# Moving the row-threshold add of a fused attention and FFN kernel from GpSimd to VectorE, with an order of instructions drawn from sixty

## Chip, cores and metric

One core of a Trainium2 chip. The metric is device time in microseconds of one execution; less is better.

## The reference, cut to what matters

```python
# q, k, v: 8 batches, 8 heads, 576 positions, 64 wide;  tau = 0.02
scores = scale * q @ k^T
thresh = max(scores, axis=-1) - tau
scores = where(scores >= thresh, scores, -1e9)
attn   = softmax(scores) @ v
# then an FFN on the 4608 rows: RMS norm, silu(x @ w_gate) * (x @ w_val) @ w_out
```

Only the threshold of each row, its maximum less tau, is touched by the change. It decides which scores survive.

## The kernel before

The kernel describes its work as a list of operations with an engine, an estimated cost, a priority and dependences. A small simulation in the kernel, `order_ops`, plays them through and gives the order in which every engine gets its instructions. I call the end time that this simulation arrives at the *reckoning*. There are 144 steps, each with the scores of two heads for 128 rows. The part of a step that matters (cut):

```python
def emit_softmax(s, so):
    for h in range(2):                      # VectorE: scores out of PSUM, negated and scaled, row minimum into mx
        nc.vector.tensor_tensor_reduce(out=ssb[a][:, h], in0=s_ps[h][...], in1=zrow, scale=-1.0 / 8.0,
                                       scalar=3.0e38, op0=ALU.add, op1=ALU.min, accum_out=mx[m][:, h:h + 1])
    def nthr(o):                            # GpSimd: the threshold of both heads, 128x2
        nc.gpsimd.tensor_scalar(out=nth[m], in0=mx[m], scalar1=tau, scalar2=None, op0=ALU.add)
    tn = add("POOL", COST["pool_tiny"], s - 4, [ttr_of[s, 0], ttr_of[s, 1]], nthr)
    # way "p", ScalarE: prelu(bias=nth) with a huge slope, then exp
    # way "g" (one head of every other step from step 16 on): ScalarE exp(bias=nth) into esb,
    #     GpSimd "mask" wsb = (ssb <= nth), GpSimd "take" wsb = wsb * esb
    ...
...
seq = order_ops(ops, {"R": 4})
for o in seq:
    o.fn(o)
```

`s_ps` has one buffer per head, so the next step's score matmuls wait until VectorE has copied this step's (in the trace of before a score group takes 1.17 us when nothing holds it and 1.91 us where it waits for the copy).

## Time and profile before

| | before |
|---|---|
| median | 568.11 us (567.13 to 568.92) |
| TensorE (PE), VectorE (DVE), ScalarE (ACT), GpSimd (POOL) busy | 98%, 75%, 80%, 57% |
| the threshold add | 144 on GpSimd, 220 ns each |
| score copy, mask, take | 754 ns, 1726 ns, 1278 ns each |

The groups' columns are: line, engine, operation, tiles written and read, shapes, count, then busy time in us and the mean in ns. A busy PE is not a full PE: a score group of eight matmuls counts as busy from its first to its last even when it is held in between (all of the 1.91 us above).

### The profile page before, as it was taken

Reading aid. Unit: us, or ns where it says so; the run is one execution under the profiler, and the core shown is the slowest. Engines: PE = TensorE matmul, PEld = TensorE weight load, DVE = VectorE, ACT = ScalarE, POOL = GpSimd, SP = SyncE. Lnnn points to the kernel's source line nnn. Section 1 sums busy time; section 2 is a strip of 40 time slices with the busy share of each in tenths; the row PEclk is TensorE's granted clock in tenths of the full one; section 3 lists DMA queues with packets and bytes.
Section 4 is the critical chain, followed back from the end, with each engine's and each line's share of the span. In section 5 each row is a group of like instructions: output and inputs, shape, how many; then the busy total and the mean of one; then the engine's idle time right before and its main releaser. Section 6 shows DMA issues by size and latency. Waiting matters only on the chain.

```text
span 568.3 us, 13686 instructions
## 1 busy us (share of the span) xinstructions
PE 558.4 (98%) x5000; PEld 334.7 (59%) x5000; DVE 427.2 (75%) x1093; ACT 457.4 (80%) x739; POOL 322.4 (57%) x462
## 2 busy tenths in 40 slices
PE   8999999999999999999999999999999999999997
PEld 4666766767676555555555555545555455454674
DVE  4899977969958588758895789659875886586354
ACT  4999899999878787979898898778978897884332
POOL 2378946976747457666766658555666555551000
PEclk9999999999999999999999999999999999999999
DMA  8999998769994686999876799789887565633211
GB/s 187 250 289 282 178 195 184 161 132 202 167 202 104 136 159 149 177 177 187 178 160 148 142 186 181 161 168 162 174 167 184 88 96 86 178 81 44 84 37 38
DMA packets 270019, 88.98 MB, mean 157 GB/s; under 512 B 252544, under 2 KB 262272, under 8 KB 269952
## 3 DMA queue, kind: packets, MB, share of 16 engines
q1 hardware_dynamic: 267168, 86.02, 74.1%
q0 software_dynamic: 1600, 1.57, 1.8%
q8 instruction: 39, 0.64, 0.5%
q10 hardware_dynamic: 1184, 0.52, 0.3%
q14 instruction: 28, 0.23, 0.1%
HBM read 37.75 MB, written 9.44 MB: 83 GB/s over the span
## 4 chain that ended last, share of the span: by engine, by line
PE 89%; DVE 3%; DMA 2%; issue 2%; ACT 2%; POOL 1%; SPq 0%; DVEq 0%; POOLq 0%; ACTq 0%
PE s_ps L566 28%; PE ring L792 16%; PE ring L797 16%; PE ring L853 14%; PE ring L697 6%; PE ring L303 2%; PE ring L693 2%; DVE ssb L589 2%; DMA qkn<-in_q_dram 1%; PE s_ps L831 1%; PE s_ps L853 1%; PE ring L659 1%; PE s_ps L797 1%; PE ring L364 1%; DMA stage<-in_q_dram 1%
## 5 line engine op out<-in xcount | busy, mean ns | idle before, releaser
L589 DVE CUSTOM_DVE_ANT_0 ssb<-s_ps,zrow 128x576 f32<-128x576 f32 x288 | 207.8, 754 | 67.7 <-PE s_ps L566 60.5
L607 ACT ACTIVATE ssb<-ssb,nth 128x576 f32<-128x576 f32 x224 | 165.9, 766 | 32.4 <-POOL nth L596 32.1
L566 PE MATMUL s_ps<-qkt 64*128 64x288 f32 x1024 | 170.2, 429 | 1.4 <-DVE mx L589 1.1
L566 PEld LDWEIGHTS s_ps<-qkt 64*128 64x128 f32 x1024 | 96.2, 186 | 53.5 <-DVE mx L589 16.2
L640 POOL TENSOR_SCALAR wsb<-ssb,nth 128x576 f16<-128x576 f32 x64 | 110.5, 1726 | 9.7 <-DMA wt<-wsb 2.9
L792 PE MATMUL ring<-xnT,wg 128*128 128x512 f16 (+1 forms) x548 | 112.9, 328 | 0.4 <-DVE sl L809 0.4
L797 PE MATMUL ring<-xnT,wv 128*128 128x256 f16 (+1 forms) x544 | 111.4, 327 | 0.6 <-ACT qTv L472 0.3
L596 POOL TENSOR_SCALAR nth<-mx 128x2 f32<-128x2 f32 x144 | 31.6, 220 | 133.9 <-DVE mx L589 120.6
L809 DVE SCALAR_TENSOR_TENSOR sl<-th,ring 128x512 f32<-128x512 f32 (+1 forms) x137 | 75.9, 554 | 25.9 <-ACT th L806 24.6
L614 ACT ACTIVATE wsb<-ssb 128x1152 f16<-128x1152 f32 x80 | 92.9, 1161 | 1.9
L806 ACT ACTIVATE th<-ring 128x512 f32<-128x512 f32 (+1 forms) x137 | 66.3, 486 | 28.9 <-PE ring L792 26.4
L853 PE MATMUL ring<-wo,hf 128*128 128x512 f16 x384 | 89.3, 380 | 0.0
L645 POOL TENSOR_TENSOR wsb<-wsb,esb 128x576 f16<-128x576 f16 x64 | 81.8, 1278 | 8.8 <-ACT esb L626 4.4
L814 DVE TENSOR_TENSOR hf<-ring,sl 128x256 f16<-128x256 f32 (+1 forms) x136 | 75.9, 558 | 10.0 <-PE s_ps L566 0.5
L797 PEld LDWEIGHTS <-wv 128*128 128x128 f16 x576 | 52.2, 98 | 42.9 <-issue 12.3
L792 PEld LDWEIGHTS <-wg 128*128 128x128 f16 x576 | 52.0, 98 | 41.0 <-issue 11.6
L853 PEld LDWEIGHTS <-hf 128*128 128x128 f16 x408 | 37.4, 98 | 47.2 <-issue 6.6
L626 ACT ACTIVATE esb<-ssb,nth 128x576 f16<-128x576 f32 x64 | 49.2, 768 | 7.1 <-POOL nth L596 7.0
L697 PE MATMUL ring<-va,wt 128*128 128x65 f16 (+1 forms) x1264 | 52.8, 193 | 0.0
L697 PEld LDWEIGHTS <-wt 128*128 128x128 f16 (+1 forms) x1280 | 48.7, 100 | 3.4
L611 ACT ACTIVATE wsb<-ssb 128x576 f16<-128x576 f32 x64 | 43.6, 681 | 1.6
L693 PE MATMUL ring<-va,wt 128*128 128x130 f16 (+1 forms) x158 | 35.1, 227 | 0.1
(68 smaller groups left out, 448.1 us busy)
## 6 DMA issues: line engine op xcount, KB each, us to landing
vst<-in_v_dram SPq DMA_DIRECT2D x32, 256.0 KB, 3.2
qkn<-in_k_dram SPq DMA_DIRECT2D x31, 256.0 KB, 3.8
out_dram<-osb SPq DMA_DIRECT2D x31, 256.0 KB, 2.6
qkn<-in_q_dram SPq DMA_DIRECT2D x28, 256.0 KB, 4.1
stage<-in_moe_w_gate_dram SPq DMA_DIRECT2D x6, 512.0 KB, 6.6
stage<-in_moe_w_val_dram SPq DMA_DIRECT2D x6, 512.0 KB, 6.3
wt<-wsb SPq DMA_TRANSPOSE x128, 3.1
wo<-in_moe_w_out_dram POOLq DMA_DIRECT2D x4, 384.0 KB, 7.6
```

What stands on the lines that cost most here:

```text
L566: nc.tensor.matmul(s_ps[h][rows, ROW_AT + n * part:ROW_AT + n * part + n], lhs(hs), kT[i][p][h][hs, n * part:n * part + n], start=True, st ...
L589: nc.vector.tensor_tensor_reduce(out=ssb[a][:, h], in0=s_ps[h][:, ROW_AT:ROW_AT + S], in1=zrow, scale=-1.0 / 8.0, scalar=3.0e38, op0=ALU.a ...
L607: nc.scalar.activation(out=ssb[a][:, h], in_=ssb[a][:, h], func=PRELU, scale=-1.0, bias=nth[m][:, h:h + 1], **PRELU_KW)
L614: nc.scalar.activation(out=wsb[s % NW], in_=ssb[a], func=AF.Exp)
L640: nc.gpsimd.tensor_scalar(out=wsb[s % NW][:, h], in0=ssb[a][:, h], scalar1=nth[m][:, h:h + 1], scalar2=None, op0=ALU.is_le)
L645: nc.gpsimd.tensor_tensor(out=wsb[s % NW][:, h], in0=wsb[s % NW][:, h], in1=esb[es], op=ALU.mult)
L697: nc.tensor.matmul(ring[o.slot[0]][rs, at:at + D + 1], w[:, 5 * h + j, rs], va[vi][:, p, 2 * j + h], start=False, stop=(h == 1 and j == 3))
L792: nc.tensor.matmul(ring[o.slot[0]][:, 0:n], wg[d][:, fs], xnT[slot][:, d, 0:n], start=(d == 0), stop=(d == 3))
L797: nc.tensor.matmul(ring[o.slot[0]][:, 0:n], wv[d][:, fs], xnT[slot][:, d, 0:n], start=(d == 0), stop=(d == 3))
L809: nc.vector.scalar_tensor_tensor(out=sl[i][:, 0:n], in0=th[i][:, 0:n], scalar=1.0, in1=ring[g.slot[0]][:, 0:n], op0=ALU.add, op1=ALU.mult)
L814: nc.vector.tensor_tensor(out=hf[hi][:, 0:n], in0=ring[vv.slot[0]][:, 0:n], in1=sl[i][:, 0:n], op=ALU.mult)
L853: nc.tensor.matmul(ring[(first or o).slot[0]], hf[hs[fc][0]][:, 128 * j:128 * (j + 1)], wo[:, fc], start=(fc == 0), stop=(fc == NFC - 1))
```

## The change

The intent: take 31.6 us and a queue off the path from row maximum to ScalarE, and find a better order by drawing.

```diff
-    sp=480.0, sp_v=650.0, sp_w=600.0, sp_tr=1300.0, sp_qk=900.0, sp_tl=630.0,
+    sp=420.0, sp_v=600.0, sp_w=600.0, sp_tr=1300.0, sp_qk=680.0, sp_tl=630.0,
...
+def best_order(ops, ring_sizes):
+    given = [o.prio for o in ops]
+    found = []
+    for seed in list(range(ORDERS)) + [None]:
+        rnd = random.Random(min(found)[1] if seed is None else seed)
+        for o, prio in zip(ops, given):
+            o.prio = prio + (rnd.gauss(0.0, 0.25) if prio > -15 else 0.0)
+        seq = order_ops(ops, ring_sizes)
+        found.append((max(o.end for o in ops), seed))
+    return seq
...
-        def nthr(o):
-            nc.gpsimd.tensor_scalar(out=nth[m], in0=mx[m], scalar1=tau, scalar2=None, op0=ALU.add)
-        tn = add("POOL", COST["pool_tiny"], s - 4, [ttr_of[s, 0], ttr_of[s, 1]], nthr)
+        tns = []
+        for lo, hi in ((0, 1), (1, 2)) if NTH == "EACH" else ((0, 2),):
+            def nthr(o, lo=lo, hi=hi):
+                (nc.gpsimd if NTH == "POOL" else nc.vector).tensor_scalar(
+                    out=nth[m][:, lo:hi], in0=mx[m][:, lo:hi], scalar1=tau, scalar2=None, op0=ALU.add)
+            tns.append(add("POOL" if NTH == "POOL" else "DVE", COST["pool_tiny"] if NTH == "POOL" else NTHC, s - 4, ...))
...
-    seq = order_ops(ops, {"R": 4})
+    seq = best_order(ops, {"R": 4})
...
+ORDERS = 60
+NTH = 'DVE'
+NTHC = 80.0
```

So three things change at once: the engine of the add, the draw, and the issue costs that the reckoning gives to DMAs.

More of the change, by code (lines that the diff above doesn't have):

```diff
@@ L123, in order_ops @@
     return out
+def best_order(ops, ring_sizes):
+    import random
+    given = [o.prio for o in ops]
[7 more added lines that the diff above has]
+    return seq
 @with_exitstack
@@ L593, in emit_softmax @@
             ttr_of[s, h] = add("DVE", COST["ttr"], s - 1, [so, o_c] + exp_of.get(s - NSS, []), ttr)
-        def nthr(o):
-            nc.gpsimd.tensor_scalar(out=nth[m], in0=mx[m], scalar1=tau, scalar2=None, op0=ALU.add)
-        tn = add("POOL", COST["pool_tiny"], s - 4, [ttr_of[s, 0], ttr_of[s, 1]], nthr)
+        tns = []
[3 more added lines that the diff above has]
+                    out=nth[m][:, lo:hi], in0=mx[m][:, lo:hi], scalar1=tau, scalar2=None, op0=ALU.add)
+            tns.append(add("POOL" if NTH == "POOL" else "DVE", COST["pool_tiny"] if NTH == "POOL" else NTHC, s - 4,
+                           [ttr_of[s, h] for h in range(lo, hi)], nthr))
         wfree = [w_read.get(s - NW)]
@@ L614, in ex2 @@
                     nc.scalar.activation(out=wsb[s % NW], in_=ssb[a], func=AF.Exp)
-                pls.append(add("ACT", COST["prelu"], s + 0.5, [tn], prelu))
+                pls.append(add("ACT", COST["prelu"], s + 0.5, [tns[h % len(tns)]], prelu))
                 if ways != "pp":
@@ L627, in ex @@
                                          bias=nth[m][:, h:h + 1])
-                e = add("ACT", COST["exp1"], s + 0.4, [tn, pre.get(("es", es))], ex)
+                e = add("ACT", COST["exp1"], s + 0.4, [tns[h % len(tns)], pre.get(("es", es))], ex)
                 if way == "d":
@@ L646, in take @@
                                                 op=ALU.mult)
-                    mk = add("POOL", COST["mask_g"], s + 0.4, [tn] + wfree, mask)
+                    mk = add("POOL", COST["mask_g"], s + 0.4, [tns[h % len(tns)]] + wfree, mask)
                     st = add("POOL", COST["take_g"], s + 0.4, [e, mk], take)
```

## The prediction

> **What bounds the kernel now.** I read the page from the top: busy shares, the chain that ended last, then the busy time by stretches, and last the groups, the waits and the timeline for the operation that moves.
>
> ```profile
> span 568.3 us, 13686 instructions
> PE 558.4 (98%) x5000; PEld 334.7 (59%) x5000; DVE 427.2 (75%) x1093; ACT 457.4 (80%) x739; POOL 322.4 (57%) x462
> ...
> PE 89%; DVE 3%; DMA 2%; issue 2%; ACT 2%; POOL 1%; SPq 0%; DVEq 0%; POOLq 0%; ACTq 0%
> ```
>
> TensorE is busy for 98% and holds 89% of the chain. GpSimd, from which the change takes work, holds 1% of the chain. A busy PE need not be a full PE, so I looked at stretches next.
>
> ```profile
> 0.00:80.00 80.00, 75.11 (x718) 52.04 (x722) 65.93 (x191) 67.22 (x107) 47.08 (x88) 1.00 1.05 233
> 80.00:180.00 100.00, 99.02 (x1059) 68.70 (x1058) 79.04 (x222) 87.96 (x155) 68.92 (x94) 1.00 0.86 168
> 180.00:510.00 330.00, 329.98 (x2853) 179.62 (x2852) 251.43 (x614) 281.84 (x437) 203.48 (x275) 1.00 0.77 153
> 510.00:568.30 58.30, 54.29 (x377) 34.37 (x375) 30.84 (x70) 20.33 (x43) 2.93 (x6) 0.99 0.20 52
> ```
>
> The columns are the stretch, its length, then the busy time of PE, PEld, DVE, ACT and POOL. From 180 to 510 us PE has no idle time at all. To see whether that is real work, I took from the timeline the start-to-start time of each group of matmuls (eight for scores, four for a gate or value, six for an output, eighteen for attention times values) and compared it with the shortest tenth of the same kind followed by the same kind of work. The excess, counted where it is over 60 ns, is 18.0 us in all: 12.4 us of it starts before 80 us, 3.4 us from 80 to 180 us, and only 2.1 us in the whole rest. So from 180 us PE is truly full, and what an ordering can win lies almost all in the first seventh. There the chain of waits shows it directly:
>
> ```profile
> 18.33 1.91 PE s_ps L566 x8
> ...
> 42.25 1.91 PE s_ps L566 x8
> 47.53 1.91 PE s_ps L566 x8
> ...
> 259.56 1.17 PE s_ps L566 x8
> ```
>
> A score group takes 1.17 us when nothing holds it, 1.91 us where the second head's matmuls wait for VectorE to copy the second head's scores of the step before out of PSUM. Early in the kernel VectorE also copies the weight transposes and transposed keys, so it is the pace-maker there (65.9 of 80 us busy).
>
> Last, the operation that moves and who waits for it:
>
> ```profile
> L596 POOL TENSOR_SCALAR nth<-mx x144: 215/220/227, 10.6 to 511.5; 128x2 f32<-128x2 f32 x144
> ...
>   ACT ssb L607: 32.1, 39
>   ACT esb L626: 7.0, 13
>   POOL wsb L640: 1.6, 2
> ```
>
> The threshold costs GpSimd 144 x 0.220 = 31.6 us, and ScalarE idles 39.1 us in 52 places for it. No PE line is among the waiters: what is lost here is ScalarE's time, and ScalarE is 80% busy.
>
> [...] The trace has near relatives: the accumulator read of one column takes 83 ns, a reciprocal of 128x4 from PSUM 179 ns. I estimate[...] 100 ns taken from the queue. [...] the score copies are uniform (747 to 759 ns) whatever GpSimd does.
>
> **The change part by part.**
>
> Part 1, off GpSimd: -31.6 us of its 322.4 (57% to 51%), and the add no longer queues behind GpSimd's mask (1.73 us) and take (1.28 us). GpSimd isn't on the path except in a few places; one is near 169 us, where the chain runs through mask and take, and PE's attention group at 175 us is 0.84 us late. Worth to the end: at most that 0.8 us, of which I count 0.3.
>
> Part 2, on to VectorE: [...] After 80 us this is hidden: from 80 to 510 us VectorE is busy for 79.0 + 251.4 = 330 of 430 us, so 100 us are free[...]. Before 80 us it isn't: 24 of the steps lie there and VectorE paces the scores; 24 x 0.1 = 2.4 us, of which I count 1.4 us as not covered by waits that it already has.
>
> Part 3, the shorter path from maximum to ScalarE. In the timeline of an undelayed step the accumulator read ends at 259.20, the GpSimd add runs from 259.37 to 259.59, and ScalarE starts at 259.62: 0.42 us. [...] Where GpSimd was occupied the wait is longer: the maximum is there at 251.83, the add starts at 253.96, and ScalarE has idled 0.63 us. Of 39.1 us of ScalarE's waits I expect 25 us to go. On the end this counts only before 80 us, where those waits sum to 4.5 us and ScalarE is busy for 67 of 80 us: I count -1.7 us.
>
> Part 4, the order. Sixty draws with shifts of a quarter of a step (3.9 us pitch, so about 1 us), and the shortest by the ordering's own reckoning. Its reckoning also gets cheaper issue costs for the loads. From 80 us on PE has 5.5 us of stalls to win, before it 12.4 us. Changes between the scores' half-array matmuls and the full-array ones cost some 0.19 us per round trip (scores to gate 335 ns against 235 ns to transposes, gate to scores 309 against 216 ns); there are 132 round trips, and I don't expect more than five to vanish (1 us). The order before was itself tuned, so a draw is on average somewhat worse, and choosing the best of sixty turns that round as far as its reckoning resembles the chip. I count -2.0 us.
>
> Part 5, unchanged: the 7.2 us to the first scores, which wait for loads, and the 4.0 us after the last matmul (564.3 to 568.3), which are an eviction and a store.
>
> Sum: -0.3 + 1.4 - 1.7 - 2.0 = -2.6 us; 568.1 - 2.6 = 565.5 us. The floor for any order of this work is 568.1 - 18.0 = 550.1 us, at 3.2% below, so 2% would need 11.4 of 18 us.
>
> **The rivals.**
>
> Rival A[...]. At the end of the second score copy GpSimd was running something other than the threshold in 16 of 24 steps before 80 us, with 0.33 us to go on the mean over all, and in 47 of 119 later, with 0.18 us. If the add waits each time, VectorE loses 7.9 us before 80 us and 21.5 us after. The latter fits into the 100 us that are free. The former brings VectorE to 65.9 + 2.4 + 7.9 = 76 of 80 us, and with the pacing there I expect 3 to 5 us on the end: 569 to 571 us. [...]
>
> Rival B, the order wins most of the slack: with early score groups at 1.2 to 1.4 us in place of 1.9 us, some 9 us of the 12.4 go and the time is 558 to 560 us. For it: the slack is of the sort that order decides (which copy VectorE takes first). Against it: the copies have to be done all the same, and VectorE is 82% busy there.
>
> Rival C, the reckoning's best isn't the chip's: it knows transfers only as fixed times, while DMA shares are about 1.05 before 80 us. One load a little later stalls PE, as the 1.0 us at 37.4 us does now (transposes held by a load of queries). That gives 568 to 572 us.
>
> **Range and chances.** A chance of a quarter for A and C together and of a sixth for B puts 8 in 10 between 560 and 571 us. Faster by over 2% means below 556.8 us, slower means above 579.5 us; PE's full stretch makes both unlikely: 0.05 faster, 0.92 within 2%, 0.03 slower.
>
> **What would show it.** In the changed trace: no GpSimd threshold, and 144 VectorE ones[...] or a long tail up to 1.7 us where GpSimd is busy (rival A). ScalarE's waits for the threshold near 14 us (part 3). PE's idle time before 80 us below 4.9 us and fewer score groups at 1.9 us (part 4); 180 to 510 us as full as before. I am wrong if PE's stretch after 180 us gets holes, if the round trips change by tens, or if the time before 80 us lengthens.

In the +1.4 us, the 100 ns of VectorE's queue per add are the estimate, set between the 83 and the 179 ns of the two relatives in the trace. Rival A is the case that the add on VectorE waits for the GpSimd instruction that is running.

## More of the kernel before

All runs quoted are fast, with a granted TensorE clock of 0.995 to 1.000. The four calls of experiments ran on four chips (numbers 12, 8, 15 and 5), so kernels of different calls are best compared by their ratios to the kernel before, which ran in every call.

Line numbers differ between the kernels: the add is L596 before and L613 (L614 with a line more) in the later ones.

## The result, and the profile after

The changed kernel takes 573.01 us (572.11 to 574.53, 6 runs) against 568.08 us (6 runs): ratio 1.0092, 95% interval 1.0072 to 1.0113. Ratios here are the mean time of one kernel's fast runs over that of the other's of the same rounds, so not quite the ratio of the medians. It is slower by 0.9%, outside the range of the prediction.

The page of the changed kernel, its head:

```profile
span 571.3 us, 13626 instructions
...
PE 552.9 (97%) x5000; PEld 330.2 (58%) x5000; DVE 456.0 (80%) x1237; ACT 460.1 (81%) x739; POOL 290.6 (51%) x318
```

GpSimd lost 31.8 us as planned. VectorE gained 456.0 - 427.2 = 28.8 us, 200 ns for each of the 144 adds, where the forecast's sum counted 100 ns. The instructions that write or read the threshold tile, and who waited for them:

```profile
L613 DVE TENSOR_SCALAR nth<-mx x144: 158/170/1072, 10.3 to 512.2; 128x2 f32<-128x2 f32 x144
...
  POOL wsb L659: 74.3, 33
  ACT ssb L626: 25.1, 40
  PEld s_ps L581: 11.2, 27
...
  ACT esb L645: 5.6, 14
```

The three durations are shortest, median and longest: the usual add takes 170 ns, but the longest takes 1072 ns for two elements per partition. ScalarE's waits for the threshold fell only from 39.1 to 25.1 + 5.6 = 30.7 us, where I had expected 14. GpSimd's mask now waits 74.3 us for the add, since it no longer follows an add of GpSimd's own; this alone costs nothing to be seen, as the split run below, which is faster, has 81.6 us of it. Of the 144 adds 33 take over 250 ns; what all adds take over 170 ns sums to 11.6 us. In the instruction records 31 of these 33 end just after a GpSimd instruction ends (21 to 26 ns after), and the two others (504 and 500 ns) run under a DMA issue of GpSimd. This is one of the 31, in order of time, with start and duration in us:

```profile
150.45 1.28 POOL L664 TENSOR_TENSOR wsb<-wsb,esb 128x576 f16<-128x576 f16 x1 [0.32 <-ACT esb L645]
...
150.70 1.05 DVE L613 TENSOR_SCALAR nth<-mx 128x2 f32<-128x2 f32 x1
150.89 1.24 PE L581 MATMUL s_ps<-qkt 64*128 64x288 f32 x8
...
151.66 0.17 DVE L733 RECIPROCAL rz<-ring 128x4 f32<-128x4 f32 x1
...
151.87 0.42 DVE L734 TENSOR_TENSOR xsb<-ring,rz 128x256 f32<-128x256 f32 x1
...
152.35 0.60 PE L816 MATMUL ring<-xnT,wv 128*128 128x256 f16 x4 [0.22 <-DVE xsb L734]
```

GpSimd's take runs from 150.45 to 151.73. The add starts at 150.70, ends at 151.75, and holds VectorE's queue. The normalisation of attention (`xsb`) frees a PSUM buffer only at 152.29, and PE, done with its scores, waits for it and starts the next group at 152.35, 1.46 us after the scores began.

Not every GpSimd instruction holds the add. 40 adds start under one that has more than 200 ns to run: 33 are held, one starts 2 ns after GpSimd's instruction and takes 197 ns, and the other six all lie under `ir`, a power of one element per partition; they take 169 to 171 ns with 278 to 391 ns of the power left. Why these did not wait is open; the spans of GpSimd's instructions are rough in the profile. One of the six:

```profile
213.66 0.57 POOL L750 TENSOR_TENSOR ir<-irm,mhalf 128x1 f32<-128x1 f32 x1
213.84 0.17 DVE L613 TENSOR_SCALAR nth<-mx 128x2 f32<-128x2 f32 x1
```

The busy time by stretches (PE, PEld, DVE, ACT and POOL after the stretch's length):

```profile
0.00:80.00 80.00, 69.55 (x710) 49.05 (x711) 68.56 (x208) 67.21 (x105) 41.45 (x64) 1.00 1.02 229
80.00:180.00 100.00, 97.05 (x1032) 66.03 (x1031) 84.41 (x248) 87.90 (x152) 59.42 (x61) 1.00 0.85 168
180.00:510.00 330.00, 328.99 (x2875) 179.53 (x2874) 269.49 (x708) 282.42 (x437) 184.88 (x187) 1.00 0.75 153
```

After 180 us PE is nearly as busy as before (329.0 against 330.0 us). But a busy PE is not a full PE, and the two kernels have different orders, so this table can't say where the time is lost; the split run in call 1, which has the order of the changed kernel, can. (The profiled run of before was one of its slower ones, 570.2 us; hence 3.0 us between the spans of the two traces, against 4.9 us between the medians.) The idle time before 80 us, 10.4 against 4.9 us, overstates the loss there: this order holds score groups before their first matmul (idle, 6.6 against 0.5 us after the first 8 us) where the old one held more of them in the middle (busy). Later runs show how little that number is worth: the fastest kernel below is idle for 8.3 us there.

### The profile page after: what moved, and what is told of

Same layout as the page of the kernel before. It is cut to its first block, busy times and chain, and to the rows that moved or that the text cites. A ratio compares the mean times of both kernels' runs of the same rounds, so it can differ in the third digit from the quotient of the medians.

```text
span 571.3 us, 13626 instructions
## 1 busy us (share of the span) xinstructions
PE 552.9 (97%) x5000; PEld 330.2 (58%) x5000; DVE 456.0 (80%) x1237; ACT 460.1 (81%) x739; POOL 290.6 (51%) x318
## 4 chain that ended last, share of the span: by engine, by line
PE 55%; DVE 8%; issue 1%; DVEq 0%; ACT 0%
PE s_ps L581 15%; PE ring L872 11%; PE ring L811 10%; PE ring L816 9%; DVE ssb L604 4%; PE ring L716 3%; DVE sl L828 2%; DVE hf L833 1%; PE s_ps L816 1%; PE ring L318 1%; PE ring L712 1%; PE s_ps L850 1%; PE s_ps L872 1%; DVE nth L613 0%; PE s_ps L811 0%
## 5 line engine op out<-in xcount | busy, mean ns | idle before, releaser
L626 ACT ACTIVATE ssb<-ssb,nth 128x576 f32<-128x576 f32 x224 | 166.1, 768 | 26.0 <-DVE nth L613 25.1
L659 POOL TENSOR_SCALAR wsb<-ssb,nth 128x576 f16<-128x576 f32 x64 | 110.5, 1727 | 131.0 <-DVE nth L613 74.3
L581 PE MATMUL s_ps<-qkt 64*128 64x288 f32 x1024 | 162.7, 429 | 8.8 <-DVE mx L604 8.3
L581 PEld LDWEIGHTS s_ps<-qkt 64*128 64x128 f32 x1024 | 91.2, 186 | 60.3 <-DVE mx L604 24.0
L811 PE MATMUL ring<-xnT,wg 128*128 128x256 f16 (+1 forms) x564 | 114.5, 325 | 0.8 <-DVE xsb L734 0.6
L816 PE MATMUL ring<-xnT,wv 128*128 128x512 f16 (+1 forms) x520 | 108.2, 330 | 0.6 <-DVE qkt L465 0.3
L828 DVE SCALAR_TENSOR_TENSOR sl<-th,ring 128x256 f32<-128x256 f32 (+1 forms) x141 | 76.6, 544 | 20.6 <-ACT th L825 20.3
L825 ACT ACTIVATE th<-ring 128x256 f32<-128x256 f32 (+1 forms) x141 | 67.6, 480 | 30.6 <-PE ring L811 26.4
L833 DVE TENSOR_TENSOR hf<-ring,sl 128x512 f16<-128x512 f32 (+1 forms) x130 | 73.6, 566 | 10.3 <-PE ring L816 0.5
L613 DVE TENSOR_SCALAR nth<-mx 128x2 f32<-128x2 f32 x144 | 36.0, 250 | 4.9
```

What stands on the lines that cost most here:

```text
L581: nc.tensor.matmul(s_ps[h][rows, ROW_AT + n * part:ROW_AT + n * part + n], lhs(hs), kT[i][p][h][hs, n * part:n * part + n], start=True, st ...
L626: nc.scalar.activation(out=ssb[a][:, h], in_=ssb[a][:, h], func=PRELU, scale=-1.0, bias=nth[m][:, h:h + 1], **PRELU_KW)
L659: nc.gpsimd.tensor_scalar(out=wsb[s % NW][:, h], in0=ssb[a][:, h], scalar1=nth[m][:, h:h + 1], scalar2=None, op0=ALU.is_le)
L811: nc.tensor.matmul(ring[o.slot[0]][:, 0:n], wg[d][:, fs], xnT[slot][:, d, 0:n], start=(d == 0), stop=(d == 3))
L816: nc.tensor.matmul(ring[o.slot[0]][:, 0:n], wv[d][:, fs], xnT[slot][:, d, 0:n], start=(d == 0), stop=(d == 3))
L828: nc.vector.scalar_tensor_tensor(out=sl[i][:, 0:n], in0=th[i][:, 0:n], scalar=1.0, in1=ring[g.slot[0]][:, 0:n], op0=ALU.add, op1=ALU.mult)
```

## The experiments

**Theory 1:** the add on VectorE costs, through its place in VectorE's queue and through a wait for the GpSimd instruction that is running (the prediction's rival A; 33 of 144 adds over 250 ns in the changed kernel). **Theory 2 (rival):** the new order costs. Within theory 1 the two parts have to be told apart. Cuts in the expectations take out how that wait was said to come about, which no run shows; an alternative that opens with a cut is the one for this wait. "Before" is measured again in every call; its medians are 568.67, 567.89, 568.38 and 568.07 us in the four calls in the order below.

### Call 1: engine and order crossed, the split, and no draw

**The old order with the add on VectorE.** The queues of PE, ScalarE and the DMA issuer stay as they were, instruction for instruction.

```diff
-            nc.gpsimd.tensor_scalar(out=nth[m], in0=mx[m], scalar1=tau, ...)
+            nc.vector.tensor_scalar(out=nth[m], in0=mx[m], scalar1=tau, ...)
```

> The order of the kernel before, every other engine's queue unchanged; only the threshold add is given to VectorE at its place in that order. Theory 1 (the add on VectorE is what costs: some 0.2 us of VectorE's queue each[...]): slower than before by 3 us or more, 571 to 574 us, add's mean near 250 ns with some over 600 ns. Theory 2 (the new order is what costs): within 1 us of before, 567 to 569 us.

Measured: 570.59 us, ratio 1.0030 (1.0007 to 1.0053). The add costs 1.9 us in the old order too. That lies between what I had set for the two theories (3 us or more, and at most 1 us): the direction is theory 1's, the size isn't. 31 adds take over 250 ns, the longest 1284 ns.

**The new order with the add on GpSimd.**

```diff
-                (nc.gpsimd if NTH == "POOL" else nc.vector).tensor_scalar(
+                nc.gpsimd.tensor_scalar(
```

> The order of the changed kernel, kept as it is on all engines, but the threshold add issued to GpSimd. Theory 1 (the add on VectorE costs): faster than the changed kernel by 3 us or more, 566 to 570 us. Theory 2 (the order costs): stays at 572 to 574 us, and PE's idle time from 80 to 180 us stays near 3 us.

Measured: 568.78 us, ratio 0.9997 (0.9970 to 1.0023). With the add back on GpSimd the new order is as good as the old one. Theory 2 falls: within the interval of 0.3% the order as such costs nothing, and gains nothing either.

**The new order, two adds of one column each on VectorE.** Nothing else moves.

```diff
-                (nc.gpsimd if NTH == "POOL" else nc.vector).tensor_scalar(
-                    out=nth[m][:, lo:hi], in0=mx[m][:, lo:hi], scalar1=tau, scalar2=None, op0=ALU.add)
+                for c in range(lo, hi):
+                    nc.vector.tensor_scalar(
+                        out=nth[m][:, c:c + 1], in0=mx[m][:, c:c + 1], scalar1=tau, scalar2=None, op0=ALU.add)
```

> The changed kernel with each threshold add made as two adds of one column, back to back, in the same place of the same order. [...] If the wait[...] is what costs (11.5 us over all adds in the changed kernel), the long adds vanish (none over 250 ns) and the time falls by 1 to 4 us to 569 to 572 us, though 144 more instructions are issued. If VectorE's queue time is what costs, the time rises by 1 to 3 us to 574 to 576 us.

Measured: 569.63 us, ratio 1.0016 (0.9994 to 1.0038). With 144 instructions more the kernel is 3.4 us faster than the changed one by the medians, 4.3 us by the ratios. Its adds:

```profile
L614 DVE TENSOR_SCALAR nth<-mx x288: 142/151/155, 10.3 to 508.5; 128x1 f32<-128x1 f32 x144
```

The longest of 288 is 155 ns, and the last add starts at 508.5 us in place of 512.2 us. The same place of the same order as shown above:

```profile
149.20 1.28 POOL L665 TENSOR_TENSOR wsb<-wsb,esb 128x576 f16<-128x576 f16 x1 [0.17 <-ACT esb L646]
...
149.52 0.27 DVE L614 TENSOR_SCALAR nth<-mx 128x1 f32<-128x1 f32 x2
149.70 0.17 DVE L734 RECIPROCAL rz<-ring 128x4 f32<-128x4 f32 x1
149.79 1.24 PE L581 MATMUL s_ps<-qkt 64*128 64x288 f32 x8
...
149.91 0.42 DVE L735 TENSOR_TENSOR xsb<-ring,rz 128x256 f32<-128x256 f32 x1
...
150.96 0.61 PE L817 MATMUL ring<-xnT,wv 128*128 128x256 f16 x4
```

The take runs from 149.20 to 150.48, and the two adds go through beneath it in 0.27 us. PE's next group starts 150.96 - 149.79 = 1.17 us after its scores began, without a wait: 0.29 us less than in the changed kernel.

PE has the same order of matmuls in this run and in the changed kernel, so the two traces can be compared matmul by matmul. The changed kernel is 0.8 us behind at 80 us, 2.3 us at 180 us, 3.3 us at 250 us and 3.5 us at the end. So the waits cost time all along: 0.8 us before 80 us, 1.5 us up to 180 us, and 1.2 us after it, where PE looks full.

**The changed kernel without the draw.**

```diff
-    seq = best_order(ops, {"R": 4})
+    seq = order_ops(ops, {"R": 4})
```

> The changed kernel without the draws: priorities as written, one pass of the ordering with the add on VectorE and the new issue costs. The ordering's own reckoning gives it 567.1 us against 566.2 us for the drawn one and 569.3 us for the kernel before. If the draw costs: 567 to 570 us, faster than the changed kernel. If the add on VectorE costs in any order: 571 to 575 us.

Measured: 572.89 us, ratio 1.0068 (1.0039 to 1.0097), 34 adds over 250 ns. The draw, reckoned to be worth 0.9 us, is worth nothing to be seen, and without it the kernel is as slow. Two adds of this run that began 55 and 170 ns into a DMA issue of GpSimd took 170 ns each, so such an issue did not always hold the add.

### Call 2: the old order split, and the draw by itself

**The old order with the split add.**

```diff
-            nc.gpsimd.tensor_scalar(out=nth[m], in0=mx[m], scalar1=tau, scalar2=None, op0=ALU.add)
+            for c in range(2):
+                nc.vector.tensor_scalar(
+                    out=nth[m][:, c:c + 1], in0=mx[m][:, c:c + 1], scalar1=tau, scalar2=None, op0=ALU.add)
```

> The order of the kernel before with the threshold on VectorE as two adds of one column. With one add of two columns this order gave 570.6 us, 1.9 us over the kernel before. If the wait[...] is most of that, as it was in the order of the changed kernel (3.4 of 4.2 us): no add over 250 ns and 568.7 to 569.6 us. If in this order VectorE's queue time is what costs: 570.5 to 572 us.

Measured: 566.81 us, ratio 0.9983 (0.9968 to 0.9998). Better than either theory had it: without the long waits the move to VectorE is a gain of about 1 us in the old order.

**The draw alone, its shortest order and its longest.**

```diff
-NTH = 'DVE'
+NTH = 'POOL'
```

> The draw alone: threshold left on GpSimd, new issue costs, the shortest of sixty orders by the ordering's own reckoning (565.8 us; the kernel before is reckoned at 569.3 us). If the reckoning is right about orders: 564 to 566 us, faster than before by 0.4 to 0.7%. If it can't tell orders apart at this size: 567 to 571 us.

```diff
-        rnd = random.Random(min(found)[1] if seed is None else seed)
+        rnd = random.Random(max(found)[1] if seed is None else seed)
-NTH = 'DVE'
+NTH = 'POOL'
```

> The same with the longest of the sixty, reckoned at 573.0 us, 7.2 us more than the best. If the reckoning tells orders apart: 571 us or more, at least 4 us slower than the run of the best. If it doesn't: within 2 us of it.

Measured: 565.92 us, ratio 0.9966 (0.9951 to 0.9981), and 570.32 us, ratio 1.0044 (1.0029 to 1.0059). With the add on GpSimd the reckoning does tell orders apart: 7.2 us reckoned between the two, 4.4 us measured. The shortest is the fastest kernel, and beats both the kernel before and the changed one:

```profile
span 563.4 us, 13656 instructions
...
PE 549.1 (97%) x5000; PEld 329.3 (58%) x5000; DVE 427.5 (76%) x1093; ACT 458.5 (81%) x739; POOL 322.2 (57%) x462
```

VectorE and GpSimd work as long as in the kernel before (427.2 and 322.4 us); the gain is in order alone.

**One add per head, the change's own other setting**, placed after each head's copy by a draw of its own.

```diff
-NTH = 'DVE'
+NTH = 'EACH'
```

> The changed kernel's own other setting: one add of one column per head on VectorE, each right after its own score copy, and the shortest of sixty orders drawn for that (reckoned 568.8 us). [...]

Measured: 575.18 us, ratio 1.0140 (1.0121 to 1.0158). I had set 568 to 571 us if the wait for GpSimd was the main cost of the changed kernel, and 573 us or more if two places in VectorE's queue per step cost more than that wait. This is slower than the changed kernel though its longest add is 157 ns. So the wait for GpSimd is not all that can go wrong with adds on VectorE. The time lies in the second range, and VectorE is busy for 465.2 us, against 451.0 us in the split run. But the run differs from the split one in order and in the place of the adds, and I can't say how much is due to which.

### Call 3: controls, and a third order

**Two adds over both columns, back to back**, as a control to the split.

```diff
                 for c in range(lo, hi):
                     nc.vector.tensor_scalar(
-                        out=nth[m][:, c:c + 1], in0=mx[m][:, c:c + 1], scalar1=tau, scalar2=None, op0=ALU.add)
+                        out=nth[m], in0=mx[m], scalar1=tau, scalar2=None, op0=ALU.add)
```

> The control to the split run: in the same order and place two adds back to back, but each over both columns (the second writes the same values again). As many instructions as in the split run (569.6 us), only with two elements per partition. [...] long adds are back (some over 600 ns, at least 30 over 250 ns) and the time is 573 to 576 us. If splitting helped for another reason (more instructions between the accumulator read and the next copy): 568 to 571 us.

Measured: 597.59 us, ratio 1.0512 (1.0496 to 1.0528). The long adds are back (55 over 250 ns, up to 2232 ns, 26.2 us over 170 ns each), but 24 us is far more than expected, and the control was not clean: the second add writes the tile that the first one wrote and starts only some 35 ns after the first has ended, in every step. It shows that VectorE's queue is sensitive, not how much the wait for GpSimd costs. It was made again below.

**The shortest order with GpSimd, with the add on VectorE: as one add and split.**

```diff
-                (nc.gpsimd if NTH == "POOL" else nc.vector).tensor_scalar(
+                nc.vector.tensor_scalar(
-NTH = 'DVE'
+NTH = 'POOL'
```

> The shortest order with the add on GpSimd (565.9 us on the chip), now with one add of two columns on VectorE at its place. [...] 568 to 571 us, 2 to 5 us slower than with GpSimd. If the earlier difference belonged to the two other orders: 565 to 567 us.

The split run has the loop over columns as in call 1, in this order.

> The same order with two adds of one column on VectorE: the candidate for the fastest version. In the order of the kernel before this was 1.1 us faster than GpSimd, in the order of the changed kernel 0.9 us slower. [...] 564.5 to 567 us, at least 2 us below the run with one add of two columns.

Measured: 570.10 us, ratio 1.0031 (1.0016 to 1.0046), and 567.21 us, ratio 0.9977 (0.9963 to 0.9992). 32 adds of the first take over 250 ns, none of the second. In a third order, too, two columns at once cost about 3 us more than one at a time, and the split form ends close to GpSimd's 565.92 us but not below it.

**The order of the one-add-per-head run, with these adds on GpSimd.**

```diff
-                (nc.gpsimd if NTH == "POOL" else nc.vector).tensor_scalar(
+                nc.gpsimd.tensor_scalar(
-NTH = 'DVE'
+NTH = 'EACH'
```

> The order drawn for one add per head (575.2 us on VectorE), with the same adds issued to GpSimd. If the two separate adds cost in VectorE's queue (each holds it some 0.2 us between the copies): 569 to 572 us, 3 us or more faster. If the order itself is what made that run slow: 574 us or more.

Measured: 596.21 us, ratio 1.0482 (1.0462 to 1.0501). It is inconclusive on what it was made for: with 288 adds on GpSimd, in places chosen for VectorE, ScalarE now waits for GpSimd, which the threshold tile's waiters show.

```profile
  ACT ssb L626: 88.0, 105
  ACT esb L645: 9.1, 15
```

97 us of waits in place of 39 us before. That is a new cost, so nothing follows about the order on VectorE.

### Call 4: a clean control, the issue costs, and an honest price

**A second add of two columns into a tile that nobody reads.**

```diff
+    spare = [sb(f"spare{i}", [128, 2]) for i in range(6)]
...
+                nc.vector.tensor_scalar(out=nth[m], in0=mx[m], scalar1=tau, scalar2=None, op0=ALU.add)
+                nc.vector.tensor_scalar(out=spare[m], in0=mx[m], scalar1=tau, scalar2=None, op0=ALU.add)
```

> A cleaner control than the double add, whose second instruction had to wait for the first (it wrote the same tile, some 35 ns plus the first one's whole time). Here the second add of two columns writes a spare tile that nobody reads, so it depends on nothing new. Same order, same number of instructions as the split run (569.6 us), only two elements per partition. [...] adds over 250 ns are back, 573 to 580 us. If splitting helped for another reason than the number of elements: 568 to 571 us, at the split run's time.

Measured: 576.95 us, ratio 1.0165 (1.0143 to 1.0186).

```profile
L614 DVE TENSOR_SCALAR nth<-mx x144: 160/170/951, 10.1 to 517.1; 128x2 f32<-128x2 f32 x144
...
L616 DVE TENSOR_SCALAR spare<-mx x144: 154/161/623, 10.2 to 517.2; 128x2 f32<-128x2 f32 x144
```

The order, the places and the number of instructions are those of the split run; that one has 288 adds of at most 155 ns and takes 569.63 us, this one has adds up to 951 ns and is 7.3 us slower by the medians, 8.5 us by the ratios. So the number of elements per partition is what matters here, not the splitting. The changed kernel is 4 us faster than this control; the long waits hardly differ (13.0 against 11.6 us over 170 ns each), so I put that down to the second add's own time in the queue, which no run shows by itself.

**The draw with the old issue costs.** The add is on GpSimd.

```diff
-    sp=420.0, sp_v=600.0, sp_w=600.0, sp_tr=1300.0, sp_qk=680.0, sp_tl=630.0,
+    sp=480.0, sp_v=650.0, sp_w=600.0, sp_tr=1300.0, sp_qk=900.0, sp_tl=630.0,
-NTH = 'DVE'
+NTH = 'POOL'
```

> The add on GpSimd, sixty draws, but with the issue costs of the kernel before: reckoned best 568.1 us (with the new costs 565.8 us reckoned, 565.9 us on the chip). If the new costs are what makes the draw useful: 567.5 to 569 us. If the draw by itself is: 565 to 567 us.

Measured: 567.99 us, ratio 1.0006 (0.9985 to 1.0028). The draw with the old costs gains nothing; with the new costs it gained 0.34%.

**The split add, its order drawn with 200 ns as the price of the pair.**

```diff
-NTHC = 80.0
+NTHC = 200.0
```

together with the split loop of call 1.

> The ordering told what the add takes of VectorE's queue on the chip (200 ns in place of 80 ns), the order drawn anew with that, and the add made as two of one column. Reckoned 569.9 us. If the wrong price of the add in the reckoning was part of the loss: 566 to 568.5 us, below the split run in the changed kernel's order (569.6 us). If not: 569 to 571 us.

Measured: 570.03 us, ratio 1.0050 (1.0023 to 1.0077). A dearer add in the reckoning did not give a better order; my first alternative was wrong. But it did give a true forecast, as the table shows.

| kernel | add | price in the reckoning | reckoned us | measured us |
|---|---|---|---|---|
| before | GpSimd | 270 ns | 569.3 | 568.1 |
| old costs, drawn | GpSimd | 270 ns | 568.1 | 568.0 |
| new costs, shortest | GpSimd | 270 ns | 565.8 | 565.9 |
| new costs, longest | GpSimd | 270 ns | 573.0 | 570.3 |
| changed kernel | VectorE, 128x2 | 80 ns | 566.2 | 573.0 |
| changed, no draw | VectorE, 128x2 | 80 ns | 567.1 | 572.9 |
| one add per head | VectorE, 128x1 twice | 80 ns each | 568.8 | 575.2 |
| split, drawn anew | VectorE, 128x1 twice | 200 ns for both | 569.9 | 570.0 |

Where the add is on GpSimd, the reckoning is right to within 2.7 us and mostly to 1.2 us. Where it is on VectorE at 80 ns, it is 6 to 7 us too low.

## Why the prediction was wrong

**The cause, in three orders.** Each column has one order; each row differs from the next in the form or engine of the add alone. The figures are ratios to the kernel before.

| add | old order | changed kernel's order | shortest GpSimd order |
|---|---|---|---|
| GpSimd, 128x2 | 1 | 0.9997 | 0.9966 |
| VectorE, two of 128x1 | 0.9983 | 1.0016 | 0.9977 |
| VectorE, one of 128x2 | 1.0030 | 1.0092 | 1.0031 |
| last row less the second | 0.47%, 2.7 us | 0.76%, 4.3 us | 0.54%, 3.1 us |

The move by itself (second row less first) is worth -1.0, +1.1 and +0.6 us: about even, at the edge of what the runs resolve. It is the move in its split form, which takes 248 ns of VectorE's queue per step where it follows an accumulator read (the instruction of 83 ns that brings the row minimum into `mx`) and nothing holds it, against 195 ns for the single add; so the last row is, if anything, too small for the wait itself. What makes the changed kernel slow is that its adds of two elements per partition wait for GpSimd (33 of 144 over 250 ns, none of 288 in the split form), 2.7 to 4.3 us at the end.

**The bound (right).** PE still sets the end; some 5 us is what it lost to VectorE's delays. Where, was wrong: against the split run in the same order, 0.8 of 3.5 us are lost before 80 us, where rival A had all of it, and 1.2 us after 180 us, where I had called the loss hidden.

**Part 1 (right in what it removes).** GpSimd lost 31.8 us.

**Part 2 (the step that failed).** "I count 1.4 us" was the VectorE term, and the wait for GpSimd was left out of the sum. Parts 1 to 3 together gave the move -0.6 us, and part 4 gave the order -2.0 us. Measured in this order: 1.1 us for the move without the wait, which holds the shorter path of part 3 as well, plus 4.3 us for the wait; the order itself gave -0.2 us. The instruction was mis-sized too: it takes 170 ns, and straight after an accumulator read the next VectorE instruction starts 195 ns after that read's start (median of 86 such adds that did not wait), where without an add it starts at once (within 5 ns for 230 of the 288 reads in the trace of before); the sum counted 100 ns. And "after 80 us this is hidden" did not hold, as 2.7 of the 3.5 us lost to the wait come after 80 us: in the example at 150 us VectorE has free time later, but PE waits now. An average of free time doesn't hide a wait of 1 us between an order's two neighbours.

**Part 3 (too optimistic).** 8.4 us of ScalarE's waits went, not 25, since the add now waits on VectorE. In the split form, too, ScalarE waits 25.5 us. Part of this is the order: with the add on GpSimd the same order has 44.0 us of such waits (41.5 + 2.5), so the move itself took away 13.3 us, and in the split form 18.5 us. The -1.7 us on the end was never separated from the move as a whole, which came out even.

**Part 4 (right for the draw, wrong for this draw).** "-2.0 us" is what the draw gave with the add on GpSimd (565.92 us). In the changed kernel it gave nothing: the same order with the add on GpSimd is at 0.9997. The draw had been judged by a reckoning with the add at 80 ns and no wait in it. That this is why it chose badly is argued, not shown: at 200 ns the drawn order was no better (570.03 us).

**Rival A (right, and underweighted).** It named the wait, the tail by which it would show and its size (3 to 5 us; 4.3 us measured). The tail to 1072 ns is there. But that the size fits is partly luck: it came from 7.9 us of waits before 80 us, and the five long adds there sum to 1.5 us over 170 ns each. In all it overstated the waits (29 us if every add that meets a busy GpSimd waits; 11.6 us measured). Its 569 to 571 us was reckoned on a gain by order that did not come. I gave A and C together a quarter, though by the prediction's own count GpSimd was busy at the end of the second copy in 63 of 143 steps. The profile of before did not show that an add would wait, so the weight was a judgement, and it was too low.

**Rivals B and C.** B's large gain by order did not come; the best drawn order took 2 us in all, where 12.4 us of slack lay before 80 us alone. C's load that comes late was not seen as the cause: with the same DMA queue order the split run and the GpSimd run are fast.

**What the marks were worth.** The long tail of the adds was the right mark. PE's idle time before 80 us was a bad one, as the fastest kernel has more of it than the kernel before.

**Still open:** why one add per head is so slow (575.2 us), and why the same 11.6 to 14.0 us of long waits cost from 2.7 to 4.3 us in different orders; where in an order they fall must matter, but no run varied that alone.

## What to carry to other kernels

A tiny VectorE instruction is not cheap because it is small: here a two-element add took 195 ns of the queue where it followed the accumulator read that it depends on (83 ns for the read, then 35 ns to the add's start). Ask what it reads, what it must wait for, and what GpSimd runs meanwhile. In this kernel, where GpSimd is busy for 51% of the span, 31 of 144 two-element SBUF-to-SBUF adds on VectorE ended 21 to 26 ns after the GpSimd instruction that ran, the longest after 1072 ns; one element at a time avoided that here (288 adds, at most 155 ns). And a search over orders is as good as the prices in its simulation: check one drawn order on the chip with each engine choice before trusting the shortest.
